# Linear attention followed by an MLP: q's second half loaded before w_out's products, k^T v one block later, one turn of q earlier

## The chip, the cores and the metric

One core of a Trainium2 chip runs the whole program. The metric is device time in microseconds (us) of an execution; several executions of each kernel were timed, and the kernel before was always timed on the same chip in the same rounds. All timed executions with a state were in the fast state; single ones are of unknown state. A profile is one further execution with the hardware profiler on; its span is 1.8 us shorter than the time of its run.

## The reference

```python
kv  = np.einsum('bhsd,bhse->bhde', k, v)             # 8 batches, 8 heads, 576 x 64
out = np.einsum('bhsd,bhde->bhse', q, kv)
rms = np.sqrt(np.mean(out * out, axis=-1, keepdims=True) + 1e-06)
x   = (out / rms * g_norm)                           # bridged to (4608, 512)
h   = x @ w_in                                       # 512 x 2048
g   = s * np.maximum(h, 0) ** 2 + b
y   = g @ w_out                                      # 2048 x 512
```

All of it is float32.

## The kernel before

The 4608 tokens are worked through in nine units (u = 0 to 8) of four chunks of 128 tokens. A unit has two products: h = x w_in (`mm1`, four steps s) and g w_out (`mm2`). Both are done with seven products of half-size blocks in place of eight. From unit 2 on, five of mm2's seven are split so once more. While unit u is multiplied, the attention of unit u + 1 (turn q, multiply by k^T v, normalize, turn x) is slipped between the blocks, and the q of unit u + 2 is loaded.

What the argument needs of it:

```python
# q for two chunks: many small transfers, 32 partitions x (n x 32) floats each
for w, b, j, n in pieces:                    # 1 to 3 pieces -> 16, 32 or 48 transfers
    for h in range(H):
        for a in range(2):
            rest.append(partial(nc.sync.dma_start, out=to[rows, h // 2, w : w + n, :],
                                in_=src[h, :, j : j + n, a * 32 : a * 32 + 32]))

# w_out's tiles (and k, v of the next batch) come through a ring of 7 buffers, on the same queue
def pump(k): ...                             # issues the next k tiles on nc.sync

# one chunk of attention (c >= 9)
def turn():     nc.vector.transpose(out=st["qT"], in_=q_in[c])
def product():  ...                          # TensorE: qT x bd_kv;  ACT: square;  DVE: sum
def norm():     ...                          # ACT: rms;  DVE: reciprocal, multiply
def turn_x():   ...                          # DVE: transpose;  for odd chunks ACT: 4 scalings by g

# where they stand: (s, n) is a place in mm1, a number or ("q", n) one in mm2
def sides(u):
    ...
    if u in kv_due:
        first[1, 2] = [lambda: kv_product(kv_due[u]), lambda: pump(NP)]
    ...
    if u == 2:
        second = {0: [turn[3], product[3]], 1: [norm[3]], 2: [turn_x[3]]}
    for n, fn in enumerate(loads_in_parts(u + 2, 1, 8)):
        second["q", n + 2] = [fn]

# one step of mm1
at(0); a["x1"](); x3(steps[s - 1]); a["z2"]()
at(1); y4(steps[s - 1]); a["x6"]()           # x6 and x5 end in a copy of x_ps on ACT ("r")
at(2); a["y7"]()
at(3); a["x5"]()
```

The timelines of this case show each queue in order: what stands ahead in the SyncE queue is issued first, and what stands ahead on ScalarE (ACT) or VectorE (DVE) is done first. `PEld` is TensorE's weight loads; `x_ps`, `y_ps`, `z_ps` and `t_ps` are the banks in which products add up, `r` a copy of one; `bd_kv` holds k^T v block by block, as the factor of q. Line 671 and 674 issue w_out's tiles, 1206 and 1217 q's transfers (1198 and 1209 in the changed kernel), 377 is k^T v, 439 q times k^T v, 91 all larger matmuls, 587 the copy of x_ps.

## Time and profile before

| | before |
|---|---|
| time, three runs | 958.37 us (954.94 to 959.96) |
| span of the profile | 955.3 us |
| PE busy, weight loads busy | 98%, 88% |
| bytes moved | 158.46 MB, 166 GB/s |

The table of DMA issues of the page (queue, count, size, median us from issue to landing) shows what kind of transfer is at issue:

```profile
w_sb<-w SPq DMA_DIRECT2D x147, 512.0 KB, 4.8
...
q_sb<-in_q_dram SPq DMA_DIRECT2D x144, 32.0 KB, 3.2
...
q_sb<-in_q_dram SPq DMA_DIRECT2D x64, 16.0 KB, 3.3
q_sb<-in_q_dram SPq DMA_DIRECT2D x64, 8.0 KB, 3.7
```

A few hundred small q transfers share a queue with w_out's tiles, which are 16 to 64 times as large. In unit 3 the queue's timeline (start, duration, what was issued) reads:

```profile
373.84 10.50 SPq L1206 DMA_DIRECT2D q_sb<-in_q_dram  x16
404.56 0.34 SPq L671 DMA_DIRECT2D w_sb<-w  x1
408.07 3.83 SPq L674 DMA_DIRECT2D w_sb<-w  x2
412.48 3.89 SPq L671 DMA_DIRECT2D w_sb<-w  x3
416.47 3.74 SPq L1217 DMA_DIRECT2D q_sb<-in_q_dram  x6
421.30 1.24 SPq L671 DMA_DIRECT2D w_sb<-w  x2
```

The first line is q's first half. Then the queue is empty until the ring has a free buffer for w_out at 404.56, and from 416 on q's second half comes in small groups between the tiles.

### The profile page before, as it was taken

What the parts mean: (1) busy time and instruction counts of PE and PEld (TensorE: products, weight loads), DVE (VectorE), ACT (ScalarE), POOL (GpSimd) and SP (SyncE); (2) the same over time, 40 slices, a digit from 0 to 9 for tenths busy, and PEclk for the clock granted to TensorE, in tenths of its full rate; (3) what the DMA queues carried; (4) which work ended last, traced back from release to release, by engine and by line L of the source; (5) the groups of instructions that cost most, each with busy time, mean ns of one, the idle gap of its engine ahead of it and who ended that gap; (6) DMA issues with size and microseconds to landing.
All of it is one profiled execution on the core that took longest, in us unless ns stands there. A gap on an engine that the chain in (4) does not pass through costs nothing.

```text
span 955.3 us, 17799 instructions
## 1 busy us (share of the span) xinstructions
PE 938.2 (98%) x7270; PEld 838.4 (88%) x7270; DVE 643.9 (67%) x1167; ACT 192.3 (20%) x366; POOL 6.7 (1%) x18
## 2 busy tenths in 40 slices
PE   7999999999999999999999999999999999999997
PEld 7888888888888998899889988989889988998997
DVE  2789767585557765786568665875678667864684
ACT  3674132101231103200231013101320032001100
POOL 2000000000000000000000000000000000000000
PEclk9999999999999999999999999999999999999999
DMA  9688827578762767066724854285607630653064
GB/s 249 202 295 248 264 80 193 137 239 254 201 165 73 214 183 200 10 198 183 205 78 126 247 159 131 87 248 163 166 22 231 187 103 12 203 179 127 13 220 143
DMA packets 136656, 158.46 MB, mean 166 GB/s; under 512 B 77696, under 2 KB 91776, under 8 KB 136448
## 3 DMA queue, kind: packets, MB, share of 16 engines
q1 hardware_dynamic: 133472, 155.57, 55.2%
q10 hardware_dynamic: 2784, 1.77, 0.8%
q8 instruction: 57, 0.93, 0.4%
q14 instruction: 23, 0.19, 0.1%
q0 software_dynamic: 320, 0.00, 0.0%
HBM read 131.34 MB, written 25.95 MB: 165 GB/s over the span
## 4 chain that ended last, share of the span: by engine, by line
PE 88%; DMA 5%; DVE 3%; ACT 2%; issue 1%; SPq 1%; ACTq 0%; DVEq 0%
PE x_ps L91 40%; PE y_ps L91 26%; PE z_ps L91 9%; PE t_ps L91 7%; PE x_ps L439 3%; DMA w_sb<-w 2%; PE kv_ps L377 2%; DMA w_raw<-in_moe_w_in_dram 1%; DMA kv_sb<-in_k_dram 1%; ACT xT L489 1%; DVE sub L250 1%; DVE xn L458 1%; DVE xT L483 1%; ACT bd_kv L392 0%; DMA w<-w_sb 0%
## 5 line engine op out<-in xcount | busy, mean ns | idle before, releaser
L587 ACT COPY r<-x_ps 128x512 f32<-128x512 f32 x96 | 56.2, 586 | 438.7 <-PE x_ps L91 396.9
L91 PE MATMUL y_ps<-xs,wb 128*128 128x256 f32 x512 | 122.8, 383 | 0.0
L91 PE MATMUL x_ps<-xs,ws 128*128 128x256 f32 x512 | 121.5, 380 | 0.0
L91 PEld LDWEIGHTS x_ps<-xs,ws 128*128 128x128 f32 x512 | 96.9, 190 | 14.0 <-issue 1.0
L91 PEld LDWEIGHTS y_ps<-xs,wb 128*128 128x128 f32 x512 | 95.3, 190 | 14.7 <-issue 2.4
L91 PE MATMUL x_ps<-xT,wa 128*128 128x256 f32 x384 | 90.3, 381 | 0.1
L247 DVE TENSOR_TENSOR a<-y_ps,r 128x512 f32<-128x512 f32 x64 | 44.1, 690 | 62.2 <-ACT r L587 57.2
L91 PE MATMUL x_ps<-w_sb,a 128*128 128x256 f32 (+1 forms) x376 | 80.4, 365 | 1.9 <-DMA w_sb<-w 1.9
L91 PEld LDWEIGHTS x_ps<-xT,wa 128*128 128x128 f32 x384 | 71.8, 190 | 11.1 <-issue 1.2
L91 PEld LDWEIGHTS x_ps<-w_sb,a 128*128 128x128 f32 x376 | 66.7, 190 | 11.2 <-DMA w_sb<-w 3.1
L542 DVE SCALAR_TENSOR_TENSOR a<-a 128x512 f32<-128x512 f32 x96 | 66.4, 691 | 3.0
L91 PE MATMUL y_ps<-w_sb,sub 128*128 128x128 f32 x504 | 62.0, 275 | 0.0
L91 PE MATMUL x_ps<-xT,ws 128*128 128x256 f32 x256 | 60.9, 381 | 0.5
L91 PEld LDWEIGHTS y_ps<-w_sb,sub 128*128 128x128 f32 x504 | 60.2, 192 | 0.7
L91 PE MATMUL z_ps<-xT,wa 128*128 128x256 f32 x256 | 60.5, 379 | 0.0
L91 PE MATMUL x_ps<-w_sb,s 128*128 128x256 f32 x256 | 57.8, 380 | 0.0
L91 PE MATMUL t_ps<-w_sb,sub 128*128 128x128 f32 x448 | 54.7, 275 | 0.4 <-DVE r L702 0.4
L91 PEld LDWEIGHTS x_ps<-xT,ws 128*128 128x128 f32 x256 | 47.8, 190 | 8.2 <-ACT r L587 2.2
L91 PEld LDWEIGHTS z_ps<-xT,wa 128*128 128x128 f32 x256 | 48.6, 190 | 6.6
L91 PE MATMUL y_ps<-w_sb,a 128*128 128x128 f32 (+1 forms) x360 | 54.0, 299 | 0.0
L91 PEld LDWEIGHTS t_ps<-w_sb,sub 128*128 128x128 f32 x448 | 52.8, 192 | 1.0 <-DVE r L702 0.6
L91 PEld LDWEIGHTS x_ps<-w_sb,s 128*128 128x128 f32 x256 | 47.5, 190 | 6.0 <-issue 0.2
(139 smaller groups left out, 1239.1 us busy)
## 6 DMA issues: line engine op xcount, KB each, us to landing
w_sb<-w SPq DMA_DIRECT2D x147, 512.0 KB, 4.8
w_sb<-w SPq DMA_DIRECT2D x35, 256.0 KB, 2.8
w_raw<-in_moe_w_in_dram SPq DMA_DIRECT2D x8, 1024.0 KB, 7.9
w_raw<-in_moe_w_out_dram SPq DMA_DIRECT2D x8, 1024.0 KB, 6.0
w_sb<-in_k_dram SPq DMA_DIRECT2D x48, 144.0 KB, 3.0
w_sb<-in_v_dram SPq DMA_DIRECT2D x48, 144.0 KB, 3.0
out_dram<-o SPq DMA_DIRECT2D x104, 64.0 KB, 1.7
w<-sub SPq DMA_DIRECT2D x20, 256.0 KB, 4.2
```

Source lines behind the costliest of these rows:

```text
L91: nc.tensor.matmul(o, lhsT=lhsT, rhs=rhs, start=start, stop=stop, skip_group_check=True)
L247: nc.vector.tensor_tensor(out=o, in0=a, in1=b, op=ALU.add)
L250: nc.vector.tensor_tensor(out=o, in0=a, in1=b, op=ALU.subtract)
L377: nc.tensor.matmul(ps[r][l * HB : l * HB + HB, i, :], lhsT=kv[l][rows, 0, j, :], rhs=kv[l][rows, 1, j, :], start=(j == 0), stop=(j == R - 1),)
L439: nc.tensor.matmul(ps[32 * p : 32 * p + 32, w, :], lhsT=st["qT"][:, p, 32 * w : 32 * w + 32], rhs=bd_kv[(b if w < 2 else b1) % 2][:, p, :] ...
L458: nc.vector.tensor_tensor(out=st["xn"].rearrange("p h d -> p (h d)").rearrange("p (c h e) -> p h c e", c=KC, h=H), in0=st["x"].rearrange(" ...
L483: nc.vector.transpose(out=to, in_=st["xn"].rearrange("p h d -> p (h d)").rearrange("p (c x) -> p c x", c=KC))
L489: nc.scalar.activation(to[:, i], to[:, i], AF.Copy, scale=g_col[:, i : i + 1])
L542: nc.vector.scalar_tensor_tensor(t, t, 0.0, t, ALU.max, ALU.mult)
L587: nc.scalar.copy(st[name], src)
```

## The change

The intent is to take q's second half out from between w_out's tiles and issue it where the DMA engines have nothing to do, in mm1's last step; to put k^T v behind `norm`, so that ScalarE's bd_kv copies don't hold up the root mean square; and in unit 2 to turn q's last chunk ahead of mm2, so that its product doesn't wait for it. The diff at its core (the eleven `at(("q", n))` of mm2 become three, late in it):

```diff
         if u in kv_due:
-            first[1, 2] = [lambda: kv_product(kv_due[u]), lambda: pump(NP)]
-        place, half = ((1, 2), (u + 2, 0)) if u > 2 else (((1, 2), (2, 1)), ((2, 2), (4, 0)))[u - 1]
-        first.setdefault(place, []).append(lambda: loads(*half))
+            first[1, 3] = [lambda: kv_product(kv_due[u]), lambda: pump(NP)]
+        for *place, unit, half in (
+            [(1, 3, 2, 1)] if u == 1 else [(2, 2, 4, 0)] if u == 2
+            else [(1, 3, u + 2, 0), (3, 1, u + 2, 1)]
+        ):
+            first.setdefault(tuple(place), []).append(partial(loads, unit, half))
 ...
         if u == 2:
-            second = {0: [turn[3], product[3]], 1: [norm[3]], 2: [turn_x[3]]}
-        for n, fn in enumerate(loads_in_parts(u + 2, 1, 8)):
-            second["q", n + 2] = [fn]
+            first[3, 3] = [turn[3]]
+            second = {0: [product[3]], 1: [norm[3]], 2: [turn_x[3]]}
+            for n, fn in enumerate(loads_in_parts(4, 1, 3)):
+                second["q", n] = [fn]
```

More of the change, by code (lines that the diff above doesn't have):

```diff
@@ L981, in rest @@
             pump(2)
-            at(("q", 0))
             step["x3"]()
@@ L988, in rest @@
             pump(2)
-            at(("q", 1))
             at(0)
@@ L999, in rest @@
             pump(2)
-            at(("q", 2))
             x5_of(0, lambda: s2((2, 3)), lambda: p6["sums"]((5, 6)))
@@ L1004, in rest @@
             pump(2)
-            at(("q", 3))
             at(1)
@@ L1009, in rest @@
             pump(2)
-            at(("q", 4))
             p6[1]()
@@ L1019, in rest @@
             pump(2)
-            at(("q", 5))
             st["r2"] = rp.tile([P, 2, HN], FP32, name="or2", tag="rb")
@@ L1026, in rest @@
             pump(2)
-            at(("q", 6))
             p7[2]()
@@ L1032, in rest @@
             pump(2)
-            at(("q", 7))
             at(3)
@@ L1041, in between @@
                 pump(2)
-                at(("q", 8))
+                at(("q", 0))
                 p4[1]()
@@ L1055, in rest @@
             pump(4)
-            at(("q", 9))
+            at(("q", 1))
             y4_of(0, 3)
@@ L1059, in rest @@
             pump(2)
-            at(("q", 10))
+            at(("q", 2))
         return {"sums": p1["sums"], "rest": rest}
```

## The prediction

> **What bounds the kernel now.** I read the page's first part (busy time by engine) first:
>
> ```profile
> PE 938.2 (98%) x7270; PEld 838.4 (88%) x7270; DVE 643.9 (67%) x1167; ACT 192.3 (20%) x366; POOL 6.7 (1%) x18
> ```
>
> TensorE has matmuls open for 938.2 of 955.3 us, and no other engine is near. The change takes no matmul away, so it can gain only where the tensor engine stands still. Matmuls overlap in this trace and their ends are modelled, so I look for standstill in the weight loads (PEld), which come one per matmul: the waits of PEld, in two stretches (34 to 346 us, then 346 us to the end), from which I take the three lines that the change can touch.
>
> ```profile
> PEld x_ps L439 <- DVE qT L409: 1.8, 1, 1.8
> ```
>
> ```profile
> PEld x_ps L91 <- DMA w_sb<-w: 3.1, 3, 1.4
> PEld x_ps L91 <- ACT r L587: 2.2, 4, 0.5
> ```
>
> The numbers are us in total, times, longest. 1.8 + 3.1 + 2.2 = 7.1 us is all that this change could win: 0.7% of 958.4. The rest of the list after 34 us is "issue" (0.2 to 0.33 us at each change of matmul shape, which stays) and small change. Then I looked up each wait in the timeline. First the DMA one, in unit 3 (SPq is the queue in which SyncE issues transfers):
>
> ```profile
> 431.90 2.77 SPq L1217 DMA_DIRECT2D q_sb<-in_q_dram  x6
> ...
> 434.77 0.37 SPq L674 DMA_DIRECT2D w_sb<-w  x1
> ...
> 436.06 1.60 PEld L91 LDWEIGHTS x_ps<-w_sb,a 128*128 128x128 f32 x8
> ...
> 439.05 1.59 PEld L91 LDWEIGHTS x_ps<-w_sb,a 128*128 128x128 f32 x8 [1.39 <-DMA w_sb<-w]
> ```
>
> Six small q transfers hold the in-order queue for 2.77 us; only then is the second half of w_out's product 3 issued, and it lands 1.39 us too late. Unit 5 has the same at 642.93 us (1.32) and unit 6 at 744.56 us (0.41); these three make the 3.1. Second, the ACT one, right after k^T v of unit 3:
>
> ```profile
> 372.12 1.07 ACT L392 COPY bd_kv<-kv_ps 64x128 f32<-64x128 f32 x4 [1.88 <-PE kv_ps L377]
> 373.21 0.30 ACT L454 ACTIVATE rms<-ss,eps_col 128x8 f32<-128x8 f32 x1
> 375.25 1.70 ACT L489 ACTIVATE xT<-xT,g_col 128x256 f32<-128x256 f32 x4 [1.74 <-DVE xT L483]
> 376.98 0.59 ACT L587 COPY r<-x_ps 128x512 f32<-128x512 f32 x1
> ```
>
> ```profile
> 375.38 1.70 PEld L91 LDWEIGHTS x_ps<-xT,wa 128*128 128x128 f32 x8
> 377.62 1.59 PEld L91 LDWEIGHTS x_ps<-xT,ws 128*128 128x128 f32 x8 [0.54 <-ACT r L587]
> ```
>
> ScalarE works in order: the four bd_kv copies, which wait for k^T v, stand ahead of the root mean square; VectorE normalizes and turns only after that; the scaling of xT waits 1.74 us for it; and the copy of x_ps stands behind that. It ends at 377.57, and the next block, ready at 377.10, starts at 377.62. Units 4, 5 and 6 show the same in the chain that ended last: a 1.99 us piece at 480.22, 581.57 and 684.10. Third, the DVE one: unit 2 turns q's last chunk on VectorE at 308.39 us, straight before its product, which starts at 309.14 after 1.78 us of waiting.
>
> Last, where there is room for the q loads (columns as in the stretches view: stretch; length; PE, PEld, DVE, ACT, POOL busy; clock; DMA share; GB/s):
>
> ```profile
> 386.00:404.00 18.00, 18.00 (x117) 15.66 (x117) 13.19 (x22) 6.22 (x13) 0.00 (x0) 1.00 0.00 1
> ```
>
> In the first product's last steps the DMA engines move nothing for 18 us, in unit 3 as in units 4, 5 and 6 (1 to 4 GB/s in the same stretches there).
>
> **What the Trainium skill says.** "Perfetto Trace Analysis", Identifying the Most-Contended Engine, holds matmul busy time a poor measure and weight-load busy time a good one; here they are 98% and 88%, and the waits above show in PEld in full but in part only in PE (the 1.39 us gap is 0.99 there), so I agree and count PEld. The same page, What "DMA-bound" means, names the issuing sequencer as one thing a kernel may be bound on; at 431.90 the queue is just that, busy 0.46 us per q transfer of 8 KB. "DMA: Bandwidth & Descriptors", Anatomy of one DMA, says that waits are made by the issuing sequencer before dispatch, not by the DMA engines, and puts some 2.0 us of fixed cost on a transfer. The first is what the q transfers do to the w transfer behind them. On the second: q transfers land in 1.7 us at best and 2.8 to 3.8 in the median here, so small transfers are worth no less than that, and hiding them is a matter of place, not of size.
>
> **The change part by part.** Matmuls, copies, bytes and transfers stay the same in number; in each engine's instruction order only places differ.
>
> (a) The q loads. In units 3 to 6 the 16 to 48 transfers of q's second half leave the gaps between w_out's tiles and go into one block after the third step's second product. All three DMA waits (1.39 + 1.32 + 0.41 = 3.1 us) have q transfers just ahead of the late tile, and unit 4, whose q groups happened to fall better, has none though its compute is the same. Gain: **3.1 us**. Unit 2 keeps its loads late, in three parts of 6, 5 and 5.
>
> (b) k^T v one block later, in units 1 to 6. The root mean square now precedes the bd_kv copies, so VectorE's normalizing and turning run beside k^T v. For unit 3: k^T v starts at 369.54 + 1.73 (one block) = 371.27 and ends some 2.5 us later, at 373.8; bd_kv copies 1.07 to 374.9; xT scaling 1.70, its input long ready, to 376.65; the copy 0.59 to 377.3. The block that waited could start at 377.1 as before, so about 0.2 us of 0.54 stays. Gain: 4 x 0.35 = **1.4 us**. Units 1 and 2 had no such wait and gain nothing.
>
> (c) Unit 2's last turn, 0.70 us on VectorE, moves ahead by some 10 us, before the add of y_ps. Gain: **1.8 us**. Its cost: the copies of x_ps after it come 0.7 us later. The first of them ended at 300.25 and the matmul that overwrites its bank starts at 300.99, so the slack of 0.74 is just used up; I put 0.2 us against it.
>
> Sum: 3.1 + 1.4 + 1.8 - 0.2 = 6.1 us.
>
> **The rivals.** (1) The block of q loads delays w_out instead. Before, w_out's next tiles were issued at 404.56, 408.07 and 411 us in unit 3, each when a buffer came free. Now they stand behind q. The block can't start before the last chunk of the old q has been turned (388.45 + 0.67 = 389.1). At 0.46 us each, 16 take 7.4 us, 32 take 14.7, 48 take 22: done at 396.5, 403.8 or 411.2. By the instruction order, unit 3 has 48, units 4 and 5 have 32, and unit 6 has 16. So only unit 3 holds w_out up, by some 3 us from 408.07 to 411.5. That tile takes 4.8 us to land (the median of the 512 KB transfers), at 416.3, and product 5 wants it at 416.64. For: no margin, and the first-half block of 16 ran at 0.66 us each, behind 2 MB of w; at that pace 48 would end at 420.8 and cost 8 us of standstill. Against: that was with the DMA engines at 98% of their time, and here they are idle; and these transfers are 8 and 16 KB. I count 0.9 us on average, with a bad case of 4 to 8 us at some 10%. (2) ScalarE or VectorE keeps the third unit's wait as it is: if k^T v's copies simply move the wait by a block, (b) gives nothing: 1.4 us lost. VectorE is busy 67%, so its turns could also come in later than I drew them. (3) The transfers were hidden anyway: of some 130 q transfers moved, three caused a wait, so all of (a) is 3.1 us, whatever the traffic. This is not so much a rival as the reason why the change is worth little. (4) Unit 2's k and v tiles for unit 3 come later: its q part is now 6 ahead of three of the four, for 2 before, some 1.9 us more of queue; they were issued by 358.4 and are wanted at 371, so hidden.
>
> **Range and chances.** 6.1 less 0.9 for rival 1 is 5.2 us: 958.4 - 5.2 = 953.2 us. The runs of before scatter by 5 us (954.94 to 959.96), so a median of few may be 2 us off by chance alone; the gain itself I hold between 0 and 7.1. Together 949.5 to 957.5. A gain over 2% would be 19 us, more than all standstill after the first 34 us; a loss over 2% would need 19 us of new waits, twice the bad case of rival 1. So same is 0.98.
>
> **What would show it.** In the profile after: PEld's waits on the DMA of w_sb at 0 to 0.9 us in units 4 to 6 (a right); PEld on ACT r about 0.8 us in all, four times 0.2, with the root mean square ahead of the bd_kv copies (b right); no wait for qT in unit 2 (c right); the DMA share in unit 3's stretch from 389 to 404 well above 0, and the queue's q block there ending near 411 (rival 1 if it is near 420, with a wait for w_sb at product 5). A span of the profile of about 950 us goes with this. The prediction is wrong if the q block runs slower than 0.5 us a transfer, or if PEld shows a new wait of more than 1 us anywhere.

## The result, and the profile after

| | before | changed |
|---|---|---|
| first timing, median of 6 runs each | 958.12 us | 954.29 us (953.67 to 954.95) |
| ratio | | 0.996 (0.9939 to 0.9981) |
| span of the profile | 955.3 us | 952.7 us |

A ratio is the mean time of one kernel's fast runs over that of the other's of the same rounds, so not quite the ratio of the medians. The changed kernel is a little faster, and by the measure of 2% the same.

The waits of the weight loads after the change, first from 34 to 346 us, then from 346 us to the end (us in total, times, longest):

```profile
PEld y_ps L91 <- DVE a L247: 0.5, 1, 0.5
```

```profile
PEld x_ps L91 <- issue: 3.4, 11, 1.4
...
PEld x_ps L91 <- DMA w_sb<-w: 1.2, 1, 1.2
PEld x_ps L91 <- ACT r L587: 0.9, 4, 0.2
```

The wait for qT is gone. The four on ACT r are still four, but of 0.22 us. The waits for w_sb are one in place of three, in unit 6. Two things are new: the wait for VectorE in unit 2, and an "issue" of 1.4 us, where there was none over 0.33 after 300 us. The 1.4 us is a DMA wait in truth, as the matmul row of the timeline and the queue's tell:

```profile
387.62 24.34 SPq L1198 DMA_DIRECT2D q_sb<-in_q_dram  x48
412.06 0.38 SPq L671 DMA_DIRECT2D w_sb<-w  x1
412.54 0.85 SPq L674 DMA_DIRECT2D w_sb<-w  x2
```

```profile
416.63 3.69 PE L91 MATMUL x_ps<-w_sb,s 128*128 128x256 f32 x16 [1.24 <-DMA w_sb<-w]
```

In unit 3 the block of 48 q transfers holds the queue until 411.96. Before, w_out's two tiles for product 5 were issued as the ring freed their buffers, from 408.07; now both are issued from 412.54 on, and the product begins at 416.63 after standing still. In the other units the block is shorter and ends in time.

The block's 24.34 us are not an even pace. 47 of its 48 transfers held the queue for 0.51 us or less, mostly with a new one every 0.47 us. One alone held it for 2.03 us, and in the same stretch the DMA view has one packet of 16 KB in a queue of the kind "instruction" (queue, packets, MB, share of the engines):

```profile
395.97 2.03 SPq L1198 DMA_DIRECT2D q_sb<-in_q_dram  x1
```

```profile
q8 instruction: 1, 0.02, 4.1%
```

The second profile of the changed kernel has the same in the same place (1.28 us). Whether the packet is the cause, no run tests.

Around k^T v of unit 3, ScalarE and the weight loads now look like this:

```profile
372.64 1.07 ACT L392 COPY bd_kv<-kv_ps 64x128 f32<-64x128 f32 x4 [3.41 <-PE kv_ps L377]
373.72 1.70 ACT L489 ACTIVATE xT<-xT,g_col 128x256 f32<-128x256 f32 x4
375.45 0.58 ACT L587 COPY r<-x_ps 128x512 f32<-128x512 f32 x1
```

```profile
376.09 1.59 PEld L91 LDWEIGHTS x_ps<-xT,ws 128*128 128x128 f32 x8 [0.22 <-ACT r L587]
```

The 1.74 us in which the scaling of xT waited for VectorE are gone: it follows the bd_kv copies at once. What remains is the plain work of the copies and the scaling, which still stands ahead of the copy of x_ps.

In unit 2, VectorE and the weight loads at the start of mm2:

```profile
298.49 0.70 DVE L409 STREAM_TRANSPOSE qT<-q_sb 128x512 f32<-128x512 f32 x1
...
299.11 0.65 DVE L247 TENSOR_TENSOR a<-y_ps,r 128x512 f32<-128x512 f32 x1
...
299.82 0.73 PEld L91 LDWEIGHTS y_ps<-xs,wb 128*128 128x128 f32 x4 [0.45 <-DVE a L247]
```

The turn pushes the add, which reads a bank of y_ps, back by 0.7 us, and the matmul that overwrites that bank waits 0.45 us.

### The profile page after: what moved, and what is told of

Read it like the earlier page. It is cut to its first block, busy times and chain, and to the rows that moved or that the text cites. A ratio compares the mean times of both kernels' runs of the same rounds, so it can differ in the third digit from the quotient of the medians.

```text
span 952.7 us, 17809 instructions
## 1 busy us (share of the span) xinstructions
PE 937.2 (98%) x7270; PEld 838.7 (88%) x7270; DVE 643.7 (68%) x1167; ACT 191.7 (20%) x366; POOL 6.7 (1%) x18
## 3 DMA queue, kind: packets, MB, share of 16 engines
q10 hardware_dynamic: 2784, 1.77, 0.8%
## 4 chain that ended last, share of the span: by engine, by line
PE 91%; DMA 4%; DVE 3%; ACT 1%; issue 0%; SPq 0%; ACTq 0%; DVEq 0%
PE x_ps L91 42%; PE y_ps L91 27%; PE z_ps L91 9%; PE t_ps L91 8%; PE x_ps L439 3%; PE kv_ps L377 2%; DMA w_sb<-w 2%; DMA w_raw<-in_moe_w_in_dram 1%; DMA kv_sb<-in_k_dram 1%; DVE sub L250 1%; DMA w<-w_sb 0%; DVE xn L458 0%; DVE xT L483 0%; PE qT_ps L418 0%; ACT xT L489 0%
```

## The experiments

Twelve runs were made, in three calls on three chips: ten edited kernels, and each of the two kernels once more. All gave the right result. The kernel before had a median of 956.10, 956.22 and 956.43 us on these chips (59, 35 and 23 runs). Two theories went in. **T1**: the parts add up as the two profiles tell, with the 48-transfer block giving back a part of the gain. **T2**: the late w_out tiles of before wait by a different amount in each execution, so the 3.1 us that one profile showed is not their mean.

### Each part alone, and the changed kernel again

`a_only`: the diff without its k^T v and turn lines (cut here: the load lines, in which q's first half goes back to (1, 2) with k^T v).

```diff
-            first[1, 3] = [lambda: kv_product(...
+            first[1, 2] = [lambda: kv_product(...
-            first[3, 3] = [turn[3]]
-            second = {0: [product[3]], ...
+            second = {0: [turn[3], product[3]], ...
```

> Only the q loads move; k^T v and unit 2's last turn stay as before. Theory T1 (the three parts add up as the two profiles tell): the three waits for w_sb (3.1 us) go, the new wait at product 5 of unit 3 (1.4 us) comes, so the time falls by 1.7 us. Theory T2 (the late tiles of before wait by a different amount in every execution, and that is where before's spread of 6 us comes from): the fall is more than 1.7 us, 2 to 4 us, and the spread of the runs shrinks to that of the changed kernel, under 2 us. In the profile: four waits of 0.54 on ACT r and one of 1.8 for qT are still there.

Measured: ratio 1.0001 (0.9993 to 1.0009), median 956.41 us of 14 runs. **No gain at all.** In the profile no w_sb wait of product 3 is left in any unit, and unit 3 waits at product 5 twice, 0.49 us ("issue") and 0.68 us (DMA). Both theories' numbers missed: T1 had 1.7 us, T2 2 to 4. The waits are those that T1 names, but in time what goes and what comes balance. The spread, 955.38 to 958.21, settles nothing.

`b_only`: the kernel before with (1, 2) made (1, 3) in the k^T v line and in the load line.

> Only k^T v moves one block (with the first half of q's loads, which is issued with it). T1: four waits on ACT r of 0.22 in place of 0.54 us, so 1.3 us less; the waits for w_sb in units 3, 5 and 6 stay. T2: the same 1.3 us, and the spread stays wide as before's, 3 us or more. A rival for this part, that k^T v moved to a later block only moves its wait: no gain, and a new wait of 0.3 us or more near k^T v.

Measured: ratio 0.9998 (0.9987 to 1.001), median 955.91 us of 13 runs. The profile shows the four waits on ACT r at 0.9 us in all, for 2.2, and no new wait near k^T v, so the rival is out. The time doesn't show the 1.3 us: the interval goes from 1.0 us of loss to 1.2 us of gain, so it nearly allows it. These 13 runs spread over 6.7 us, more than any other kernel's. What k^T v's place is worth in time stays open within that interval.

`c_only`: the kernel before with unit 2's `turn[3]` at (3, 3).

> Only unit 2's last turn moves. Both theories: the wait for qT of 1.8 us goes and 0.45 us of a new wait for the add of y_ps comes, so 1.3 us less; spread as before's.

Measured: ratio 0.999 (0.9983 to 0.9998), median 955.26 us of 21 runs: 1.0 us, with an interval of 0.2 to 1.6. The profile has the new wait of 0.44 us for the add of y_ps and none for qT. As expected.

`after_again`: the changed kernel, unedited.

> The changed kernel once more, for a second profile. The wait of 1.4 us at product 5 of unit 3, the four of 0.22 on ACT r and the one of 0.45 are set by the order of instructions and come again within 0.2 us. The wait of 1.24 us for the second tile of product 3 in unit 6, whose transfer took 7.0 us with no q transfer near it: if it is a chance of the DMA it is gone or elsewhere (0 to 0.5 us); if it is a matter of order it comes again in unit 6 at over 1 us.

Measured: ratio 0.9971 (0.9963 to 0.9979), median 953.29 us of 22 runs: 2.8 us, and this is a closer measure than the first 6 runs. In its profile the four waits of 0.22 and the one of 0.44 came again. Unit 3's wait came as two of 0.68 and 0.92 us. The wait of 1.24 us in unit 6 did **not** come again: its tile was late by chance, with no q transfer near it.

The three parts alone sum to 0 + 0.2 + 1.0 = 1.2 us and together give 2.8. The half-widths of the four intervals, 0.8, 1.1, 0.7 and 0.8 us, come to 1.7 us as the root of the sum of squares, as large as that difference, so no interplay of the parts is shown.

`before_again`: the kernel before, unedited, one look.

> The kernel before once more, for a second profile. The four waits of 0.54 us on ACT r and the one of 1.8 us for qT come again. The waits for w_sb in product 3 (1.39, 1.32, 0.41 us in units 3, 5, 6) are margins of a transfer and come again in other sizes or units, 1 to 3 us in sum.

Measured: four waits of 0.53 to 0.54 us on ACT r and 1.77 us for qT, as before. The waits for w_sb are 2.2 us in sum, in another distribution (weight loads of three blocks in the timeline, units 3, 4 and 5):

```profile
439.08 1.59 PEld L91 LDWEIGHTS x_ps<-w_sb,a 128*128 128x128 f32 x8 [1.25 <-DMA w_sb<-w]
...
540.75 1.59 PEld L91 LDWEIGHTS x_ps<-w_sb,a 128*128 128x128 f32 x8 [0.46 <-DMA w_sb<-w]
...
642.47 1.59 PEld L91 LDWEIGHTS x_ps<-w_sb,a 128*128 128x128 f32 x8 [0.51 <-DMA w_sb<-w]
```

With `b_only` (one wait, 1.0 us) and `c_only` (two, 2.0 us), which have before's q loads too, four profiles give 3.1, 1.0, 2.0 and 2.2 us: 2.1 on average. That is T2's main claim, and it holds for units 4 to 6 (in unit 5: 1.32, 0, 0 and 0.51 us). Unit 3's tile was late in all four, by 1.39, 0.97, 1.34 and 1.25 us, so that one isn't chance (unit 3 has the most q transfers among the tiles, 48). T2's other half, that the spread of the times comes from these tiles, is not borne out: `after_again`, without them, spreads over 5.7 us. The times go with the granted clock, which is an association and no test: over all 117 runs of before in these calls, the 20 at 1.000 took 955.5 us in the mean and the 18 at 0.997 took 957.4.

### The long block of q transfers

`q_split`: unit 3's block cut to 32 transfers, the last 16 late in mm2.

```diff
+            else [(1, 3, 5, 0)] if u == 3
             else [(1, 3, u + 2, 0), (3, 1, u + 2, 1)]
...
+        if u == 3:
+            parts = loads_in_parts(5, 1, 3)
+            first[3, 1] += parts[:2]
+            second["q", 1] = [parts[2]]
```

> The changed kernel, but in unit 3 only 32 of the 48 transfers of q's second half stand in the block; the last 16 are issued in the second product, after the next k and v tiles. If the wait at product 5 of unit 3 (1.4 and 1.6 us in two profiles) comes from the number of transfers ahead of w_out in the queue, it is gone and the ratio to before falls from 0.997 to about 0.9955 (1.5 us). Rival: that tile is late because its own transfer is slow or its buffer is free late; then the wait stays at over 1 us.

Measured: ratio 0.9962 (0.9949 to 0.9975), median 952.84 us of 6 runs. The queue's timeline in unit 3:

```profile
387.43 16.36 SPq L1209 DMA_DIRECT2D q_sb<-in_q_dram  x32
403.89 0.37 SPq L671 DMA_DIRECT2D w_sb<-w  x1
406.36 3.83 SPq L674 DMA_DIRECT2D w_sb<-w  x2
```

The tiles are issued as the ring frees their buffers again, and no wait for w_sb is left in the whole profile. The transfers ahead in the queue made the wait. The step in time from 0.9971 to 0.9962, 0.9 us, goes the right way but is within the intervals.

`a_split`: `a_only` with the same cut.

> Only the q loads move (k^T v and the last turn as before), with the block of unit 3 cut to 32 transfers. If moving the q loads gains what the late tiles cost before (1.0 to 3.1 us in three profiles with before's loads, 2 us on average) and lost it again to unit 3's long block, this one is 1.5 to 2 us faster than before, ratio 0.998, where the same without the cut was 1.0001. Rival: the q loads among w_out's tiles cost nothing on average, ratio 1.000.

Measured: ratio 0.9981 (0.9973 to 0.9988), median 954.38 us of 18 runs. That is 1.8 us of gain, where `a_only` has none, with intervals that don't overlap. In its profile no wait for w_sb is left. So the move of the q loads is worth about 2 us, and the block of 48 took about all of it back: this is where the expected gain of that part went. The two kernels ran on two chips, each against the kernel before on its own. `a_only`'s one profile shows 1.17 us of the block's cost; the five profiles with the block of 48 show 1.17 to 2.71, 1.84 on average.

`q_doubled`: each transfer of the 32 in units 4 and 5 cut into two, with the same bytes.

```diff
-   rows = slice(32 * (2 * (h % 2) + a), ... + 32)
+   for lo in range(0, 32, 16 if c in (26, 30) else 32):   # 16 partitions each for these two
```

> The changed kernel, with each of the 32 q transfers in the blocks of units 4 and 5 cut into two of half the size: 64 transfers, the same bytes. If the number of transfers in the queue sets the delay, at 0.5 us each the blocks end near 520 and 623 us instead of 506 and 608, w_out's product 5 waits 6 to 10 us in each unit, and the kernel is 12 to 20 us slower than the changed one. If the bytes set it, the blocks end where they did and nothing changes.

Measured: ratio 1.0207 (1.0184 to 1.0231), median 977.99 us of 4 runs: slower beyond doubt, though whether by 2% is unclear. The queue and the matmuls of unit 4 (in both fences the timeline):

```profile
485.74 38.20 SPq L1200 DMA_DIRECT2D q_sb<-in_q_dram  x70
524.04 0.37 SPq L673 DMA_DIRECT2D w_sb<-w  x1
524.51 0.85 SPq L676 DMA_DIRECT2D w_sb<-w  x2
```

```profile
528.69 6.73 PE L91 MATMUL x_ps<-w_sb,s 128*128 128x256 f32 x16 [9.24 <-DMA w_sb<-w]
```

The 64 transfers and a few ahead of them take 0.55 us each, and product 5 stands still for 9.40 us of weight loads here and 9.84 in unit 5. So the number of transfers in the in-order queue sets the delay, and bytes don't: the DMA engines were at 11% from 490 to 520 us. It costs more than the 12 to 20 us expected, some 22 to 25 us against the changed kernel. The clock accounts for the rest: product 5's first 16 weight loads took 6.36 us here and 5.69 in unit 5, where the changed kernel takes 3.32. In the stretches view (length; PE, PEld, DVE, ACT, POOL busy; granted clock; DMA share; GB/s) the clock stands at half as the matmuls start again:

```profile
528.00:534.00 6.00, 5.31 (x13) 4.27 (x14) 0.00 (x0) 0.00 (x0) 0.00 (x0) 0.50 0.84 339
534.00:540.00 6.00, 6.00 (x35) 5.43 (x34) 3.56 (x7) 0.00 (x0) 0.00 (x0) 0.93 0.41 121
```

The Trainium skill's "TensorE: Matmul & The Clock Gate", What's actually happening, says that the array's clock halves after an idle window of some 3.4 us. This trace agrees: after 9.24 us of standstill the granted clock was 0.50 for the first 6 us and 1.00 in the stretch from 540 us on, and after the 1.2 us standstill in unit 3 of the changed kernel it stayed at full speed.

### The two small waits that were left

`turn_early`: unit 2's turn right after the third chunk's product.

```diff
-            first[3, 3] = [turn[3]]
+            first[3, 0].append(turn[3])
```

> The changed kernel, but unit 2's last turn stands some 10 us earlier, after the third chunk's product, where VectorE stands idle for 2 us. If the 0.45 us wait for the add of y_ps is the turn's 0.7 us ahead of it, it goes (0 to 0.1 us left) and nothing takes its place; if VectorE was late there anyway it stays.

Measured (one look, so no time is quoted): no wait for the add of y_ps is left, and none took its place in unit 2. Unit 3's product 5 waited 1.56 and 0.74 us in this profile. On VectorE the turn fills part of a gap that was 2.00 us in the kernel before:

```profile
288.88 0.70 DVE L409 STREAM_TRANSPOSE qT<-q_sb 128x512 f32<-128x512 f32 x1
290.96 0.69 DVE L621 TENSOR_TENSOR a<-a 128x512 f32<-128x512 f32 x1 [1.38 <-ACT a L618]
```

`kv_two_later`: k^T v at (2, 0), in all units.

```diff
-            first[1, 3] = [lambda: kv_product(kv_due[u]), lambda: pump(NP)]
+            first[2, 0] = [lambda: kv_product(kv_due[u]), lambda: pump(NP)]
```

> The changed kernel, but k^T v one more block later, before the third step's first product. ScalarE then scales xT and copies x_ps before it comes to the bd_kv copies. If the 0.22 us left in units 3 to 6 is those copies standing ahead of the x_ps copy, all four go: 0.8 to 0.9 us less, ratio to before about 0.996. Rival: the next copy of x_ps or the product that reads bd_kv waits instead, and nothing is won.

Measured: ratio 0.9988 (0.998 to 0.9996), median 954.84 us of 21 runs: **slower** than the changed kernel (0.9971). The four waits of 0.22 did go, but unit 1 got a new one (weight loads, timeline):

```profile
157.67 1.70 PEld L91 LDWEIGHTS y_ps<-xs,wb 128*128 128x128 f32 x8
160.87 1.59 PEld L91 LDWEIGHTS x_ps<-xs,ws 128*128 128x128 f32 x8 [1.49 <-ACT r L587]
162.79 1.31 PEld L377 LDWEIGHTS kv_ps<-w_sb 64*64 64x64 f32 x77 [0.33 <-issue]
```

In unit 1 k^T v had been filling the time in which this block waits for the copy of x_ps, as the order of the lines shows: now it comes after the wait. Unit 3's wait for w_sb was also longer in this profile, 1.28 and 1.43 us, so part of the loss can be chance there. That was one profile and was not taken further.

`combined`: the cut block, the early turn and k^T v at (2, 0).

> The three corrections together: 1.5 + 0.45 + 0.85 = 2.8 us less than the changed kernel, ratio to before about 0.994; in the profile no wait of PEld over 0.3 us after 330 us but for chance lateness of one w tile (up to 1.3 us).

Measured: ratio 0.9967 (0.9957 to 0.9977), median 952.42 us of 13 runs. That is 0.4 us better than the changed kernel and not 2.8. Unit 1's 1.49 us is there again. A chance wait of 0.91 us came at the bias row, at 100 us, which no part of this touches. After 330 us the expectation for the waits held.

`best`: the same, but k^T v at (2, 0) only where it pays.

```diff
-            first[2, 0] = [lambda: kv_product(...
+            first[(2, 0) if u > 2 else (1, 3)] = [lambda: kv_product(...
```

> The split q block and the earlier turn, and k^T v two blocks later in units 3 to 6 only, since in unit 1 that cost 1.49 us on ACT r. Expected: unit 1's new wait is gone, so 1.5 us less than the combined kernel: ratio to before about 0.995. Rival: the standstill that is left is scatter of the clock and of the start, and it comes out as the combined kernel did, 0.9967.

Measured: ratio 0.9947 (0.9935 to 0.9959), median 952.05 us of 5 runs, against 956.43 for before. Unit 1's 1.49 us is gone from its profile. This beats the kernel before by 5.1 us, and by the ratios the changed kernel (0.9963 at its best end) too; that last comparison is across two chips. From 346 us on, the weight loads' waits are now these and nothing else:

```profile
PEld x_ps L439 <- issue: 6.6, 20, 0.3
PEld x_ps L91 <- issue: 2.0, 10, 0.2
PEld y_ps L91 <- issue: 2.0, 10, 0.2
PEld kv_ps L377 <- issue: 1.3, 4, 0.3
PEld x_ps L91 <- DMA w_sb<-w: 0.6, 1, 0.6
```

The last is in unit 8, which loads no q, so late w_out tiles are not all q's doing.

## Why the prediction was right or wrong, point by point

The frame was right: the standstill of the weight loads bounds what can be won, the change is worth some us, and the time, 954.29 us, lies within the range, 1.1 us above the predicted 953.2. The gain was 3.8 us by the first timing and 2.8 by the larger one, where 5.2 was predicted. That the time came so near was partly luck: the kernel before stood at 958.4 us in the three runs that the prediction started from, and at 956.1 to 956.4 in the larger samples on other chips. Three terms of the sum were too friendly.

- **(a) The q loads, 3.1 us.** The mechanism held: in the changed kernel's two profiles no tile of product 3 waited but one, and `a_split` gained 1.8 us. The size was read from one profile. Four profiles give 2.1 on average, 1.0 us less, and only unit 3's wait is in all of them.
- **(b) k^T v, 1.4 us.** Confirmed in the trace, and closely: 0.22 us is left of each 0.54, where about 0.2 was worked out. In time it isn't resolved.
- **(c) The turn, 1.8 us less 0.2.** The wait went. Its cost was 0.45 us and fell on another instruction than the one I looked at: the slack was worked out for the copy of x_ps, but the add of y_ps ahead of it had less: in the kernel before it ended at 299.25, and the weight load that has to wait for it started at 299.36, a slack of 0.11 us.
- **Rival 1, the block ahead of w_out, 0.9 us on average.** The place was right (unit 3, product 5, and only there). The cost was 1.4 us in the first profile and 1.6 in the second. The step that failed is the length of the block: 24.34 us, where 48 x 0.46 = 22.1 was worked out, 2.3 us more. The pace of the single transfer was right (0.47 us from one to the next); the sum left no room for a stall like the one transfer of 2.03 us. It also put the margin at none, and what is left at zero margin is up to the tiles' landing: the block took 23.4 to 24.5 us in five profiles, and the wait came to 1.17 to 2.71. The block also began 1.5 us earlier than I had it, with VectorE's turn, but the product was wanted 1.4 us earlier as well, so only the length mattered. Both statements of when the prediction is wrong came true, the pace over 0.5 us by a hair and only in the mean (24.34 / 48 = 0.51), and the new wait over 1 us; both point at this term. One reading of this rival was too broad: the DMA engines' 98% holds from 373 to 378 us, but over the first-half block of 16 as a whole their share was 0.68.
- **Rival 2** did not come in the changed kernel. It came in another form when k^T v was moved once more. **Rivals 3 and 4** were as told: no wait for q or for k and v.

With the sizes as the waits show them: 2.1 + 1.3 + (1.8 - 0.45) - 1.8 = 2.9 us (an estimate from averages over few profiles), and 2.8 was measured, with an interval of 2.0 to 3.5. In the sum only (b) is not borne out by its own timing.

## What to carry to other kernels

In an in-order queue, count transfers, not bytes: a block of small ones delays whatever follows by its number times the pace of one (0.5 us here, with a stall now and then), so set its length, with a margin, by the slack until the next large transfer is wanted. When an operation is moved, look both at what it was waiting behind and at what it was covering: k^T v in the wrong place cost 1.49 us because it had been filling somebody else's wait. Where a wait is the margin of a transfer, take its size from several profiles, since one of them can be off by half.

## What the Trainium skill lacked or had wrong

- "DMA: Bandwidth & Descriptors", Anatomy of one DMA, gives about 50 ns for the sequencer's dispatch and calls descriptor generation small, but for transfers that GpSimd issues; it has no such breakdown for SyncE's. Here a q transfer of 8 to 32 KB held SyncE's queue for 0.44 us in the median.
- The same page, Issuing engines are not separate DMA queues, calls the time to initiate a DMA usually small relative to the DMA. These small transfers are an exception: in the block of 48 it was 0.43 us beside 1.7 to 1.9 from issue to landing (medians), and in `q_doubled` such blocks made the kernel 2% slower with the DMA engines at 11%. No page gives, for Trainium2 by name, the time that one small transfer issued from SyncE holds its queue.
- No page says that a transfer's issue can be slow while an "instruction" queue moves a packet. In the fourteen profiles, after 340 us, 98 q transfers held the queue for over 1 us, and 87 of these overlap in time with a 16 KB packet of such a queue; of all 2928 q transfers 174 do (counted in the traces). That is a link, not a shown cause.
- No page says that a transfer's time to land scatters enough to turn a margin into a wait: with the q loads of before, product 3's tile of 512 KB was late by 1.32, 0, 0 and 0.51 us in unit 5 in four profiles.
